# One kernel's attention stage, two chunks at a time: scores, state sums and value products of both chunks grouped by kind

## The chip, the cores and the metric

The kernel runs on one core of one Trainium2 chip. The metric is the device time of one execution in microseconds (us). Five engines of the core work side by side, each through its own instructions in order: TensorE (PE in the profile; PEld is its weight load), VectorE (DVE), ScalarE (ACT), GpSimd (POOL) and SyncE (SP), whose queue issues most of the DMAs here.

## What is computed

A gated linear attention feeds a gated feed-forward layer. Cut to what matters:

```
a = (a_re + i*a_im) * min(|a|, 0.999) / (|a| + 1e-6)
for t in range(768):                       # each of 4 batches, 8 heads, head size 48
    S = a[t][:, None] * S + outer(k[t], v[t])          # S complex, 48 x 48
    y[t] = q[t] @ real(S)
x = y rearranged to 3072 tokens x 384
h = x @ w_in                               # 384 -> 2048
out = (h * cos(h)) @ w_out                 # 2048 -> 384
```

## The kernel before

**Chunks and groups.** The 768 steps of a batch are cut into 6 chunks of 128 steps, 24 chunks in all. Two neighbouring chunks make a group, so there are 12 groups, 0 to 11. Groups 0 and 1 run by an order written out by hand. Groups 2 to 11 run in one loop, whose pass `n` holds group n's attention, group n's first product (tokens by `w_in`), the second product (by `w_out`) of group n-1, and the preparation of group n+1 (logs of the gates, their running sums over the chunk, angles, turned keys and queries).

**One chunk's attention.** `f_scores` (twice, four heads each) multiplies keys by queries into a PSUM tile `sc`; VectorE multiplies it by the causal mask into `atm`. `f_state` calls `state_sums`, 24 small products (three for each head) that fill the PSUM tile `sp`, and `state_next`, in which VectorE adds `sp` to the state of the chunk and multiplies by the decay `end` (two VectorE instructions; only one where nothing is carried into the chunk). The result is the state that the next chunk uses. `f_out` makes the chunk's values in the PSUM tile `yp`: for each pair of heads two matmuls on `atm` and, if the chunk has a state, two on the state; ScalarE then copies `yp` to `yT`. Nothing is carried into a batch's first chunk (this is the first chunk of groups 3, 6 and 9); a batch's last chunk makes no state sums (the second chunk of groups 2, 5, 8 and 11). `f_x` sends `yT` to a DRAM tile, `f_xt` brings it back as `xT`, the input of the first product.

**The logs' sums.** `log_steps` runs a chain over ScalarE and VectorE for group n+1: squares, logarithm, exponentials, a VectorE maximum-and-add into `pair`, a minimum into `lg`, a logarithm of `rs`, a subtraction into `lg`, its rounding `hi` on ScalarE and the rest `lo` on VectorE. `p_powers` (called through `prods`) sums `hi` and `lo` over the chunk by four matmuls into the PSUM tiles `lgs`; ScalarE takes exponentials of these.

**The second product** is done by seven block products (`seventh`, 8 matmuls each, in two halves of 4), in the order 0, 1, 3, 2, 5, 4, 6. `products(n-1, 0, 1)` is product 0 (PSUM tile `sum`), `products(n-1, 1, 2)` product 1 (`op`), `products(n-1, 2, 3)` product 3 (`sum`, with the left side `s2`). Product 5 follows in the same PSUM tile after ScalarE has copied product 3 out to `ot`.

**What sets the order.** `weave` takes lists of steps, each with a stretch (lo, hi) of the pass, spreads a list's steps evenly in its stretch, sorts all by place, and calls them. Every matmul goes through `matmul`, which puts it behind the one before it (line 692 of the profile): TensorE runs in exactly the woven order. In the loop the lists of VectorE and ScalarE are not fixed by hand (`Ordered.by_hand` is emptied at line 1814, except ScalarE's special functions, which are chained): the compiler's list scheduler orders them, and it was the same scheduler that filled the order seen in the trace. SP's queue is in the scheduler's order too, with a few DMAs put behind others (`behind`).

Before, `chunks(n)` has ten steps in the stretch 0 to 0.36: for each chunk two score halves, an empty step, and one step with `f_state` and `f_out`; then `f_x`, the load of `im` for group n+2 and `f_xt`; then the fetch of `end` and `v`. The logs' sums are not a list of their own: the second chunk's `f_out` calls them as `between`, ahead of its first pair of heads, or ahead of its third where the chunk is the last of a batch. Product 1's halves stand at 0.0975 and 0.1925 of the pass, one between the first chunk's scores and its sums, the other between the second chunk's score halves:

```
product 0 | sc sc | product 1 half | sp yp | sc | product 1 half | sc | sp (logs' sums) yp | product 3 ...
```

The PSUM pool `pa` has five banks; `sc`, `sp`, `yp`, `lgs`, the phases' sums and some tiles of the first product share it.

## Time and profile before

| | |
|---|---|
| median of 3 runs | 629.77 us (629.24 to 630.23) |
| the profiled execution | 629.86 us, span 628.1 us |
| granted TensorE clock | 0.998 |
| busy: PE, PEld, DVE, ACT | 608.1, 555.3, 531.8, 461.3 us |
| matmul records | 5057 |

The profile comes from one execution. Its page gives busy times by engine, the span in 40 slices, the chain that ended last, and groups of instructions; the trace behind it also answers who waited for whom, and lists instructions in order of time. A line of such a list reads: start, length, engine, line of the code, operation, output <- inputs, partitions and shape, count; in brackets the engine's idle time before it and what ended that. Neighbouring instructions of one form are merged into one line, so its length covers them all and the engine's pipelined ends overlap with the next line. Starts of neighbouring lines are therefore compared, not lengths. A matmul in full float32 is listed as two records: a score half of four heads is x8, a chunk's state sums x48, half of a block product x8.

### The profile page before, as it was taken

The page shows a single profiled execution, that of the slowest core. Times are in us where ns is not written, and L with a number is a line of the kernel's source. Part 1 is how long each engine was busy: PE and PEld are TensorE (multiplying, and loading weights), DVE is VectorE, ACT ScalarE, POOL GpSimd, SP SyncE. Part 2 cuts the span into 40 slices and gives each one's busy share as a digit, 9 for nine tenths or more (in the row PEclk, how much of TensorE's full clock was granted, in tenths as well). Part 3 has the DMA queues.
Part 4 walks back from the last instruction along what each step waited for, and adds up shares of the span by engine and source line. Part 5 has one row for each costly group of instructions (what it writes and reads, how often), then busy time and mean ns, then how long its engine had stood idle before and what let it go on. Part 6 is the DMA issues. An engine that isn't in the chain of part 4 may idle for free.

```text
span 628.1 us, 12990 instructions
## 1 busy us (share of the span) xinstructions
PE 608.1 (97%) x5057; PEld 555.3 (88%) x5057; DVE 531.8 (85%) x779; ACT 461.3 (73%) x832; POOL 28.5 (5%) x45
## 2 busy tenths in 40 slices
PE   8899999999999998998999999999999999999995
PEld 5788867776889998998999999998999999999995
DVE  6999989967898799899889989889889989982471
ACT  7888687286698597698598698598599598572440
POOL 4010110000000000000000000000000000000000
PEclk9999999999999999999999999999999999999999
DMA  9969574714937567486396496496496494371001
GB/s 235 257 185 226 166 214 79 201 46 107 226 69 187 152 148 202 125 180 176 102 223 179 111 220 175 105 218 166 121 222 174 110 228 125 104 176 52 27 0 32
DMA packets 237569, 95.04 MB, mean 151 GB/s; under 512 B 209501, under 2 KB 229726, under 8 KB 237498
## 3 DMA queue, kind: packets, MB, share of 16 engines
q1 hardware_dynamic: 229960, 68.51, 46.5%
q0 software_dynamic: 5824, 25.50, 13.1%
q8 instruction: 42, 0.69, 0.5%
q10 hardware_dynamic: 1714, 0.11, 0.2%
q14 instruction: 29, 0.24, 0.1%
HBM read 69.28 MB, written 24.81 MB: 150 GB/s over the span
## 4 chain that ended last, share of the span: by engine, by line
PE 55%; ACT 19%; DVE 13%; issue 5%; DMA 4%; SPq 2%; ACTq 0%; DVEq 0%
PE hp L692 20%; PE op L692 13%; PE sum L692 12%; PE hb L692 3%; ACT xT L681 2%; PE yp L692 2%; DVE tr L681 2%; PE phs L692 2%; ACT tan L712 2%; ACT rs L712 2%; ACT gate L712 2%; DMA kT<-moved 2%; ACT L708 2%; ACT lg L712 2%; DVE gate L681 2%
## 5 line engine op out<-in xcount | busy, mean ns | idle before, releaser
L712 ACT ACTIVATE gate<-hp,half_pi_b 128x512 f32<-128x512 f32 x96 | 68.7, 715 | 50.2 <-PE hp L692 30.3
L692 PE MATMUL hp<-xT,w_in 128*128 128x256 f32 (+1 forms) x492 | 104.9, 369 | 0.0
L692 PE MATMUL op<-w_out,gate 128*128 128x192 f32 (+1 forms) x464 | 102.3, 370 | 0.0
L692 PEld LDWEIGHTS hp<-xT,w_in 128*128 128x128 f32 x492 | 89.7, 190 | 12.6 <-issue 0.2
L692 PEld LDWEIGHTS op<-w_out,gate 128*128 128x128 f32 x464 | 78.7, 190 | 15.2 <-issue 0.4
L692 PE MATMUL hp<-xh,wh 128*128 128x256 f32 x342 | 60.8, 286 | 0.0
L681 ACT ACTIVATE xT<-hp 128x512 bf16<-128x512 f32 x96 | 60.0, 625 | 0.0
L692 PE MATMUL hp<-xl,wl 128*128 128x256 f32 x342 | 59.0, 281 | 0.0
L692 PE MATMUL sum<-w_out,gate 128*128 128x192 f32 x304 | 52.5, 326 | 0.0
L681 DVE SCALAR_TENSOR_TENSOR gate<-hp,gate 128x512 f32<-128x512 f32 x57 | 39.2, 688 | 13.0 <-ACT xT L681 12.7
L692 PE MATMUL sc<-qT,kT 96*128 96x128 f32 x384 | 49.6, 278 | 0.3 <-ACT qT L681 0.3
L692 PEld LDWEIGHTS hp<-xh,wh 128*128 128x128 f32 x342 | 49.5, 189 | 0.5
L692 PEld LDWEIGHTS sc<-qT,kT 96*128 96x128 f32 x384 | 46.7, 192 | 3.2 <-issue 1.9
L692 PEld LDWEIGHTS sum<-w_out,gate 128*128 128x128 f32 x304 | 49.5, 190 | 0.1
L692 PE MATMUL hb<-xx,wx 128*128 128x256 f32 x342 | 48.6, 282 | 0.0
L692 PEld LDWEIGHTS hp<-xl,wl 128*128 128x128 f32 x342 | 48.4, 188 | 0.0
L681 DVE TENSOR_TENSOR hp<-hp,gate 128x512 f32<-128x512 f32 x57 | 39.3, 693 | 6.8 <-PE hp L692 2.6
L692 PEld LDWEIGHTS hb<-xx,wx 128*128 128x128 f32 x342 | 44.0, 188 | 0.0
L681 ACT ACTIVATE gate<-hb 128x512 f32<-128x512 f32 x57 | 35.8, 628 | 10.8 <-PE hb L692 9.8
L692 PE MATMUL yp<-atm,v 128*48 128x128 f32 x352 | 33.8, 278 | 3.4 <-DVE atm L681 3.4
L681 DVE TENSOR_TENSOR gate<-hp,gate 128x512 f32<-128x512 f32 x39 | 26.2, 678 | 12.8 <-ACT xT L681 12.6
L681 DVE TENSOR_TENSOR atm<-sc,causal 128x512 f32<-128x512 f32 x48 | 32.3, 683 | 4.8 <-PE sc L692 4.8
(161 smaller groups left out, 1222.2 us busy)
## 6 DMA issues: line engine op xcount, KB each, us to landing
moved<-tr SPq DMA_DIRECT2D x20, 768.0 KB
raw<-in_moe_w_in_dram POOLq DMA_DIRECT2D x16, 768.0 KB, 5.7
raw<-in_moe_w_out_dram POOLq DMA_DIRECT2D x16, 768.0 KB, 5.3
kT<-moved SPq DMA_DIRECT2D x80, 96.0 KB
qT<-moved SPq DMA_DIRECT2D x20, 384.0 KB
k<-in_k_dram SPq DMA_DIRECT2D x24, 192.0 KB
q<-in_q_dram SPq DMA_DIRECT2D x24, 192.0 KB
v<-in_v_dram SPq DMA_DIRECT2D x24, 192.0 KB
```

The costliest lines, as they stand in the source:

```text
L681: ins = getattr(self.engine, op)(**kw)
L692: chain(nc.tensor.matmul(out, **kw), "tensor")
L708: chain(nc.scalar.preload_act_table_set(table))
L712: chain(nc.scalar.activation(func=func, **kw))
```

## The change

The step list `chunks` is split into lists of its own. In the pass, the four score halves of both chunks come first (places 0 to 0.05), then the state steps of both chunks (0.05 to 0.06), then the value products of both chunks and the `f_x`, `im`, `f_xt` step (0.06 to 0.09). The logs' sums become one step at 0.13 and are no longer called from within `f_out`. Product 1's halves move to 0.1125 and 0.1375, so that they stand before and after the logs' sums. The fetch of `end` and `v` keeps its place (0.342). On TensorE the order is then:

```
product 0 | sc sc sc sc | sp sp | yp yp | product 1 half | logs' sums | product 1 half | product 3 ...
```

The matmuls themselves, and every other instruction, stay as they are in number and form.

```diff
-    def f_out(n, between=lambda: None):
+    def f_out(n):
...
         for p in range(HH):
-            if p == (0 if n % NCH < NCH - 1 else 2):
-                between()
             for side in range(2):
...
-    def chunks(g):
-        for n in range(g * G, g * G + G):
-            for hh in range(2):
-                yield lambda n=n, hh=hh: f_scores(n, hh)
-            yield lambda: None
-            yield lambda n=n: (f_state(n), f_out(n, lambda: n % G and [t() for t in prods(g + 1)]))
+    def own(g):
+        return range(g * G, g * G + G)
+
+    def scores(g):
+        return [lambda n=n, hh=hh: f_scores(n, hh) for n in own(g) for hh in range(2)]
+
+    def states(g):
+        return [lambda n=n: f_state(n) for n in own(g)]
+
+    def outs(g):
+        for n in own(g):
+            yield lambda n=n: f_out(n)
         yield lambda: (f_x(g), g + 2 < NG and load(g + 2, ("im",), put=after_x), f_xt(g))
+
+    def fetches(g):
         if PEG < g + 1 < NG:
             yield lambda: (ends(g + 1), load(g + 1, ("v",), put=lambda **kw: behind(
                 nc.sync.dma_start(**kw), late["ends"])))
...
-        weave((mixes(n - 1, 1, 2), 0.0, 0.08), (logs(n + 1), 0.0, 0.02), (chunks(n), 0.0, 0.36),
+        weave((mixes(n - 1, 1, 2), 0.0, 0.08), (logs(n + 1), 0.0, 0.02), (scores(n), 0.0, 0.05), (states(n), 0.05, 0.06), (outs(n), 0.06, 0.09),
+              ([lambda: [t() for t in prods(n + 1)]], 0.13, 0.13), (fetches(n), 0.342, 0.342),
               (upper[2:] if plain else [], 0.0, 0.2), (products(n - 1, 0, 1), -0.02, -0.01),
-              (products(n - 1, 1, 2), 0.05, 0.24), (products(n - 1, 2, 3) if n < NG - 1 else [], 0.28, 0.36),
+              (products(n - 1, 1, 2), 0.1, 0.15), (products(n - 1, 2, 3) if n < NG - 1 else [], 0.28, 0.36),
```

## The prediction, on record before the changed kernel ran

> **What bounds the kernel now.** I read the page's shares first, then the waits of TensorE, then TensorE's and VectorE's instructions in order of time for one pass of the loop, then the same stretch in the other passes.

> ```profile
> span 628.1 us, 12990 instructions
> PE 608.1 (97%) x5057; PEld 555.3 (88%) x5057; DVE 531.8 (85%) x779; ACT 461.3 (73%) x832; POOL 28.5 (5%) x45
> PEclk9999999999999999999999999999999999999999
> ```

> ```profile
> PE yp L692 <- DVE atm L681: 3.4, 4, 1.1
> PE sum L692 <- ACT ot L681: 1.8, 4, 0.6
> PE lgs L692 <- DVE lo L681: 1.6, 3, 0.8
> ...
> PE lgs L692 <- ACT hi L733: 0.5, 1, 0.5
> ```

> TensorE is busy all the way (97%) at full clock (9 in every slice), so the program is TensorE's list plus its waits, and no wait of the first product (`hp`) for `xT` is among them. The rows give us in total, times, and the longest. What this change can remove is in the four rows: 3.4 us before value products, 1.6 + 0.5 us before the logs' sums, and 1.8 us before product 5 (`sum`), which waits until ScalarE has copied product 3 out. The second thing to know is how close VectorE runs behind. This is group 10's attention stage on TensorE:

> ```profile
> 513.57 1.95 PE L692 MATMUL sc<-qT,kT 96*128 96x128 f32 x16
> 515.35 1.47 PE L692 MATMUL op<-w_out,gate 128*128 128x192 f32 x8
> 516.75 0.88 PE L692 MATMUL sp<-v,ks 128*32 128x48 f32 x48
> 517.56 0.43 PE L692 MATMUL yp<-atm,v 128*48 128x128 f32 x4
> 517.82 0.39 PE L692 MATMUL yp<-qT,state 96*48 96x128 f32 x4
> ...
> 519.46 1.16 PE L692 MATMUL sc<-qT,kT 96*128 96x128 f32 x8
> 520.45 1.47 PE L692 MATMUL op<-w_out,gate 128*128 128x192 f32 x8
> 521.76 1.06 PE L692 MATMUL sc<-qT,kT 96*128 96x128 f32 x8
> 522.74 0.88 PE L692 MATMUL sp<-v,ks 128*32 128x48 f32 x48
> 523.55 0.44 PE L692 MATMUL lgs<-hi,exact 128*128 128x384 f32 x1
> ...
> 524.45 0.43 PE L692 MATMUL yp<-atm,v 128*48 128x128 f32 x4
> ...
> 526.35 2.87 PE L692 MATMUL sum<-t_s,gate 128*128 128x192 f32 x16
> ...
> 532.12 2.87 PE L692 MATMUL sum<-t_s,s 128*128 128x192 f32 x16 [0.30 <-ACT ot L681]
> ```

> and on VectorE over the same time:

> ```profile
> 515.23 0.68 DVE L681 SCALAR_TENSOR_TENSOR gate<-hp,gate 128x512 f32<-128x512 f32 x1
> 515.83 0.68 DVE L681 TENSOR_TENSOR atm<-sc,causal 128x512 f32<-128x512 f32 x1
> 516.42 0.68 DVE L681 TENSOR_TENSOR s<-gate 128x512 f32<-128x512 f32 x1
> 517.02 0.68 DVE L681 TENSOR_TENSOR atm<-sc,causal 128x512 f32<-128x512 f32 x1
> 517.63 0.68 DVE L681 TENSOR_TENSOR gate<-gate 128x512 f32<-128x512 f32 x1
> 518.23 0.95 DVE L681 SCALAR_TENSOR_TENSOR pair<-re,pair 128x768 f32<-128x768 f32 x1
> 519.09 0.55 DVE L681 TENSOR_SCALAR lg<-lg 128x768 f32<-128x768 f32 x1
> 519.56 0.54 DVE L681 SCALAR_TENSOR_TENSOR state<-sp,state 96x384 f32<-96x384 f32 x1
> 520.03 0.94 DVE L681 TENSOR_TENSOR lg<-lg,rs 128x768 f32<-128x768 f32 x1
> 520.90 0.54 DVE L681 TENSOR_TENSOR state<-state,end 96x384 f32<-96x384 f32 x1
> 521.36 0.68 DVE L681 TENSOR_TENSOR gate<-s,gate 128x512 f32<-128x512 f32 x1
> 522.15 0.96 DVE L681 SCALAR_TENSOR_TENSOR lo<-lg,hi 128x768 fp32r<-128x768 f32 x1
> ```

> No row has an idle time: VectorE is full from the last gate of the first product (515.23) on. It carries the masks (`atm`), the state, and the log chain (`pair`, `lg`, `lg`, `lo`) in one line. The first state is finished at 520.90 + 0.54 = 521.44, and its user, the second chunk's value products, comes at 524.45: three microseconds of cover, made by two score halves, half of product 1, the second state sums and the logs' sums. Group 10 has no wait in this stage; group 8, a batch's end without second state sums, has one, and group 9, whose first chunk opens a batch and carries nothing in, almost none:

> ```profile
> 419.43 1.95 PE L692 MATMUL sc<-qT,kT 96*128 96x128 f32 x16
> ...
> 429.64 0.43 PE L692 MATMUL yp<-atm,v 128*48 128x128 f32 x4 [0.96 <-DVE atm L681]
> ...
> 432.57 2.87 PE L692 MATMUL sum<-t_s,gate 128*128 128x192 f32 x16
> ```

> ```profile
> 466.89 1.95 PE L692 MATMUL sc<-qT,kT 96*128 96x128 f32 x16
> ...
> 470.88 1.08 PE L692 MATMUL yp<-atm,v 128*48 128x128 f32 x16
> 471.89 1.16 PE L692 MATMUL sc<-qT,kT 96*128 96x128 f32 x8
> ```

> **What goes.** The eight waits before `yp` and `lgs` (4 + 3 + 1) idle 3.4 + 1.6 + 0.5 = 5.5 us, and each costs a little more than its idle, since the pipeline refills: group 8's stage takes 432.57 - 419.43 = 13.14 us; group 10's 526.35 - 513.57 = 12.78 less one set of state sums (517.56 - 516.75 = 0.81) is 11.97; the difference is 1.17 for an idle of 0.96. So 5.5 + 8 x 0.2 = 7.1 us go, if nothing takes their place: the masks of the second chunk can now be made while state sums and the first value products run.

> The four waits before product 5 go too. ScalarE copies the second chunk's `yp` between the logs' sums and that point now; afterwards it has done so before. Their idle is 1.8 us; with the same refill 1.8 + 4 x 0.2 = 2.6; I take 2.5.

> Fewer changes of matmul form. After the change group 10 would take 32 score records at 1.78 for 16 (515.35 - 513.57), 3.56; a change to `sp` 0.09 (522.74 - 521.76 = 0.98 against 0.89 for half of 1.78); two state sums 1.62; two value products 1.80 and 1.90 (519.46 - 517.56 = 1.90, of which 0.1 is the change); half of product 1, 1.31 + 0.10 for its change (515.35 to 516.75 is 1.40); logs' sums 0.90 (524.45 - 523.55); the other half 1.31. Sum 12.59 against 12.78: 0.2 a group, in nine groups 1.8 us. [...]

> **What comes: a wait for the first state.** Scores of both chunks now come first, so VectorE gets four masks where it had two, ahead of the state; and the state's user comes earlier. Which of two ready instructions VectorE takes is the scheduler's choice. The rows show it taking, of what is ready, what stands earliest in the pass: the log chain (place 0.01) ahead of the state (0.126), and at 517.63 a subtraction of the mixes (place 0.15), when neither was ready. In the new pass the logs still stand at 0.01, scores to 0.044, `s` at 0.04, states at 0.0525. With the steps of the rows (a mask 0.60, `pair` 0.86, `lg` 0.47, the subtraction 0.87, the first state operation 0.47), VectorE's list becomes: mask 515.83, mask 516.43, mask or `s` 517.03 and 517.63, `pair` 518.23, `lg` 519.09, last mask 519.56, subtraction 520.16, state 521.03 and 521.50, finished 522.04. TensorE wants that state after 3.56 + 0.09 + 1.62 + 1.80 and the second chunk's first four records (517.82 - 517.56 = 0.26): 7.33 us after 513.57, at 520.90. It waits 1.1, with the semaphore 1.2 us. Behind the waiting `yp` everything on TensorE queues: the rest of the chunk, product 1, the logs' sums; ScalarE's copy to `yT` waits with it. By type of group: where the second state sums are missing (5, 8) TensorE comes 0.8 earlier and waits 2.0; where the first chunk opens a batch (3, 6, 9) its value products take 1.01 instead of 1.90 (471.89 - 470.88), TensorE comes 0.9 earlier, but the state is one operation, finished 0.46 earlier: 1.6. In 4, 7 and 10 it is 1.2. Sum 2 x 2.0 + 3 x 1.6 + 3 x 1.2 = 12.4. Group 2, with longer second products between, is not shown in such a form; between 0 and 2.0 I take 1.0, near group 10's. Group 11 prepares no logs and pays nothing. 13.4 us in all.

> **What moves at no cost.** `f_x`, five `im` loads and `xT` now stand ahead of the `re` loads on SP. The data arrive no later than before, and TensorE does not wait for `xT` today. If that cover were gone, `hp` would wait at the start of the first product. The logs' sums come after 3.56 + 0.09 + 1.62 + 3.70 + 1.41 = 10.38 us and the new wait 1.2, at 11.6; before at 9.98 (523.55). `lo` needs only 522.15 + 0.96 - 513.57 = 9.54, or a state's two operations later, so no wait is left there.

> **The sum.** 629.86 - 7.1 - 2.5 - 1.8 + 13.4 = 631.9 us. The profiled execution (span 628.1, 1.8 outside it) lies 0.1 above the median, 629.77, which changes nothing. [...]

> **The rivals.**

> *The state goes first.* If the scheduler sees the state sums ready before the log chain, the state is finished about 515.83 + 4 x 0.60 + 0.47 + 0.54 = 519.2, before TensorE asks. Then nothing takes the place of the old waits: 629.86 - 11.4 = 618.5, and about 2 back in groups 3 and 4, whose `lo` comes late (there the old waits were for `lo` and `hi`): 620.5. For it: the state operation at 519.56 went ahead of the subtraction. Against it: `pair` and `lg` are ready by 518.23 and stand earlier in the pass.

> *Only the subtraction gives way.* If at 520.16 it isn't ready yet, as it wasn't at 519.56, the state is done 0.87 earlier in eight groups: 631.9 - 7.0 = 624.9.

> *The masks come one step later.* If the scheduler believes the later scores unready at 517.63, it fills in the subtraction of the mixes as it does today, and state and masks are each 0.60 later. In eight groups that is 4.8: 636.7. It decides as soon as the third mask starts after 518.2 in group 10's time. This is the mechanism on the slow side, beside my own; waits of over 3 us it doesn't give.

> *Nothing to measure.* New waits equal to old ones in each type of group, 629.9.

> **How the numbers follow.** A measurement of this kernel tells 0.2%, 1.26 us, from no change: faster is under 628.5, slower over 631.0. My forecast has 0.43, with two to three us either way for group 2 and the early groups 3 to 5, whose VectorE rows come later than group 10's: 0.02 faster, 0.13 same, 0.28 slower. State first 0.22 and subtraction giving way 0.14, all faster; masks later 0.14, slower; nothing 0.07, same. Faster 0.38, same 0.20, slower 0.42. The forecast's own range is 629 to 634.5; the one for 8 in 10 reaches to the cases on both sides, 620 to 637.

> **What would show it.** Right: TensorE's waits list `yp` behind VectorE's `state`, eight or nine times with 1 to 2 us; `yp` behind `atm`, `lgs` behind `lo` and `sum` behind `ot` are gone or small; on VectorE the subtraction into `lg` stands ahead of the first state operation, and the last mask after `pair`. Wrong: `state` in front of `pair` or `lg`, or no wait of `yp` above 0.5 us; then the time is near 620. If `hp` or `phs` waits, a later chain has taken over that I held to be covered.

## The result, and the profile after

The changed kernel takes 637.46 us (median of 4 runs, 637.12 to 639.15); the kernel before, on the same chip, 630.00 (629.24 to 630.99). The ratio is 1.0123, with a 95% interval from 1.0100 to 1.0146: slower, by 7.5 us. The forecast was 631.9 with a range from 620 to 637, so the direction with the highest chance was right and the size lies just outside the range. The profiled execution took 637.12 us, of which 635.3 are its span.

The page of the changed kernel, its first lines:

```profile
span 635.3 us, 12981 instructions
...
PE 606.6 (95%) x5057; PEld 560.5 (88%) x5057; DVE 532.4 (84%) x779; ACT 460.2 (72%) x832; POOL 29.1 (5%) x45
...
PEclk9999999999999999998999999999999998999998
```

The work is the same (5057 matmuls) and TensorE's share fell from 97 to 95%. New are the slices with an 8 in the clock's row; the first two lie in groups 5 and 10, the third is the end of the program, behind the last matmul. TensorE's waits, in total, times, longest:

```profile
PE yp L692 <- DVE state L681: 16.1, 9, 3.0
...
PE sum L692 <- ACT ot L681: 0.9, 2, 0.5
...
PE yp L692 <- DVE atm L681: 0.3, 1, 0.3
```

This is the prediction's mechanism: the value products wait nine times for the first chunk's state. The waits for `lo` and `hi` are gone; what is left for `atm` is one of group 1, in the part ordered by hand. But the new wait is 16.1 us instead of the 13.4 that the prediction gives. Group 10 on TensorE:

```profile
518.06 3.74 PE L692 MATMUL sc<-qT,kT 96*128 96x128 f32 x32
521.73 1.56 PE L692 MATMUL sp<-v,ks 128*32 128x48 f32 x96
...
527.70 0.43 PE L692 MATMUL yp<-qT,state 96*48 96x128 f32 x4 [2.30 <-DVE state L681]
...
529.55 2.93 PE L692 MATMUL op<-w_out,gate 128*128 128x192 f32 x8
...
533.11 1.46 PE L692 MATMUL op<-w_out,gate 128*128 128x192 f32 x8
534.40 2.76 PE L692 MATMUL sum<-t_s,gate 128*128 128x192 f32 x16
```

TensorE asks for the state at 527.70 - 2.30 = 525.40, 7.34 us after the first score; the prediction had worked out 7.33. The state is what is late. The two rows of `op` are the two halves of one product with the same shape: 2.93 us in front, 1.46 behind. The first ran at half clock, as the windows below show. VectorE over the same time shows why the state is late:

```profile
519.56 1.28 DVE L681 TENSOR_TENSOR atm<-sc,causal 128x512 f32<-128x512 f32 x2
...
521.76 0.96 DVE L681 SCALAR_TENSOR_TENSOR pair<-re,pair 128x768 f32<-128x768 f32 x1 [0.32 <-ACT pair L712]
522.64 0.68 DVE L681 TENSOR_TENSOR atm<-sc,causal 128x512 f32<-128x512 f32 x1
523.24 0.55 DVE L681 TENSOR_SCALAR lg<-lg 128x768 f32<-128x768 f32 x1
523.70 0.68 DVE L681 TENSOR_TENSOR atm<-sc,causal 128x512 f32<-128x512 f32 x1
524.30 0.95 DVE L681 TENSOR_TENSOR lg<-lg,rs 128x768 f32<-128x768 f32 x1
525.17 0.54 DVE L681 SCALAR_TENSOR_TENSOR state<-sp,state 96x384 f32<-96x384 f32 x1
525.64 0.68 DVE L681 TENSOR_TENSOR gate<-gate 128x512 f32<-128x512 f32 x1
526.24 0.94 DVE L681 SCALAR_TENSOR_TENSOR lo<-lg,hi 128x768 fp32r<-128x768 f32 x1
527.11 0.54 DVE L681 TENSOR_TENSOR state<-state,end 96x384 f32<-96x384 f32 x1
```

The state stands behind `pair`, the last mask and the subtraction into `lg`, as forecast; its first operation starts 7.11 us after the first score, where the prediction's list has 7.46. Its two operations were forecast next to each other. Between them stand a subtraction of the mixes (525.64, 0.60 to the next start) and `lo` (526.24, 0.87), so the state is finished at 527.11 + 0.54 = 527.65, 9.59 us after the first score; the prediction has 8.47.

The half clock can be read from windows over the wait and over the work behind it. The columns are the stretch, its length, busy time of PE, PEld, DVE, ACT and POOL, the granted TensorE clock, and the DMAs; first group 5, then 8, then 10, each with the wait in the first row:

```profile
281.00:284.30 3.30, 0.35 (x8) 0.09 (x2) 3.30 (x7) 3.24 (x5) 0.00 (x0) 0.86 0.58 210
284.30:290.00 5.70, 5.69 (x37) 5.29 (x37) 4.19 (x6) 3.88 (x8) 0.76 (x1) 0.50 0.14 32
427.50:431.90 4.40, 1.53 (x28) 1.27 (x24) 4.40 (x8) 4.34 (x7) 0.00 (x0) 1.00 0.58 182
431.90:437.00 5.10, 5.08 (x48) 4.90 (x49) 3.95 (x5) 3.12 (x8) 0.72 (x1) 1.00 0.36 59
525.00:527.70 2.70, 0.41 (x8) 0.15 (x4) 2.70 (x6) 2.66 (x6) 0.00 (x0) 1.00 0.54 222
527.70:532.50 4.80, 4.80 (x37) 4.45 (x38) 3.22 (x5) 1.48 (x3) 0.72 (x1) 0.65 0.29 51
```

Behind the wait of group 5 (2.96 us) the clock is 0.50, behind that of group 10 (2.30) 0.65, behind that of group 8 (2.89) it stays at 1.00. From the end of the wait to product 3 group 5 takes 292.21 - 284.31 = 7.90 us where group 8 takes 437.00 - 431.92 = 5.08 for the same matmuls; group 10 takes 534.40 - 527.70 = 6.70 where group 7 takes 388.15 - 383.07 = 5.08. That is 2.8 + 1.6 = 4.4 us, more than half of the whole loss.

### The profile page after: what moved, and what is told of

It is laid out like the page before. It is cut to its first block, busy times and chain, and to the rows that moved or that the text cites. A ratio compares the mean times of both kernels' runs of the same rounds, so it can differ in the third digit from the quotient of the medians.

```text
span 635.3 us, 12981 instructions
## 1 busy us (share of the span) xinstructions
PE 606.6 (95%) x5057; PEld 560.5 (88%) x5057; DVE 532.4 (84%) x779; ACT 460.2 (72%) x832; POOL 29.1 (5%) x45
## 4 chain that ended last, share of the span: by engine, by line
PE 60%; DVE 18%; ACT 14%; issue 4%; DMA 3%; SPq 1%; DVEq 0%; ACTq 0%
PE op L692 19%; PE hp L692 18%; PE sum L692 13%; PE yp L692 3%; PE hb L692 3%; ACT gate L712 3%; ACT xT L681 3%; DVE lg L681 3%; DVE gate L681 2%; DVE tr L681 2%; DVE atm L681 2%; PE phs L692 2%; ACT L708 2%; DVE pair L681 2%; DMA kT<-moved 2%
## 5 line engine op out<-in xcount | busy, mean ns | idle before, releaser
L692 PE MATMUL op<-w_out,gate 128*128 128x192 f32 (+1 forms) x464 | 105.4, 379 | 0.0
L692 PE MATMUL hp<-xT,w_in 128*128 128x256 f32 (+1 forms) x492 | 104.9, 370 | 0.0
L692 PEld LDWEIGHTS hp<-xT,w_in 128*128 128x128 f32 x492 | 89.7, 190 | 12.5 <-issue 0.2
L692 PEld LDWEIGHTS op<-w_out,gate 128*128 128x128 f32 x464 | 81.6, 195 | 17.1 <-issue 2.0
L692 PE MATMUL hp<-xh,wh 128*128 128x256 f32 x342 | 60.8, 286 | 0.0
L692 PE MATMUL hp<-xl,wl 128*128 128x256 f32 x342 | 59.0, 281 | 0.0
L681 ACT ACTIVATE xT<-hp 128x512 bf16<-128x512 f32 x96 | 59.0, 614 | 0.0
L692 PE MATMUL sum<-w_out,gate 128*128 128x192 f32 x304 | 52.5, 326 | 0.0
L692 PEld LDWEIGHTS hp<-xh,wh 128*128 128x128 f32 x342 | 49.5, 189 | 0.5
L692 PEld LDWEIGHTS sum<-w_out,gate 128*128 128x128 f32 x304 | 49.5, 190 | 0.1
L692 PE MATMUL hb<-xx,wx 128*128 128x256 f32 x342 | 48.6, 282 | 0.0
L692 PEld LDWEIGHTS hp<-xl,wl 128*128 128x128 f32 x342 | 48.4, 188 | 0.0
L681 DVE SCALAR_TENSOR_TENSOR gate<-hp,gate 128x512 f32<-128x512 f32 x57 | 39.1, 686 | 9.9 <-ACT xT L681 9.6
L681 ACT ACTIVATE gate<-hb 128x512 f32<-128x512 f32 x57 | 35.3, 619 | 16.3 <-PE hb L692 15.3
L681 DVE TENSOR_TENSOR hp<-hp,gate 128x512 f32<-128x512 f32 x57 | 39.5, 694 | 8.6 <-PE hp L692 4.2
L692 PE MATMUL yp<-qT,state 96*48 96x128 f32 x304 | 31.1, 283 | 16.1 <-DVE state L681 16.1
L692 PE MATMUL sc<-qT,kT 96*128 96x128 f32 x384 | 45.5, 276 | 0.3 <-ACT qT L681 0.3
L692 PEld LDWEIGHTS sc<-qT,kT 96*128 96x128 f32 x384 | 44.5, 192 | 1.0 <-ACT qT L681 0.5
L692 PEld LDWEIGHTS hb<-xx,wx 128*128 128x128 f32 x342 | 44.0, 189 | 0.0
L681 ACT ACTIVATE ot<-sum 128x192 f32<-128x192 f32 x39 | 12.6, 323 | 36.3 <-PE sum L692 35.4
L681 DVE TENSOR_TENSOR gate<-hp,gate 128x512 f32<-128x512 f32 x39 | 26.3, 677 | 13.1 <-ACT xT L681 12.9
```

The lines of the kernel that those rows point to most:

```text
L681: ins = getattr(self.engine, op)(**kw)
L692: chain(nc.tensor.matmul(out, **kw), "tensor")
```

## The experiments

The prediction's own reading (Theory A) is that VectorE reaches the first state too late, because the log chain stands ahead of it. Its rivals are named in the expectations. Each kernel was timed next to the kernel before, and the ratio is to those runs.

**Logs behind the states.** In the changed kernel the log chain moves from the front of the pass to a place behind the states; TensorE's order is the changed kernel's.

```diff
-(logs(n + 1), 0.0, 0.02)
+(logs(n + 1), 0.06, 0.062)
```

> The changed kernel, with the log chain traced behind the state steps (place 0.061 instead of 0.01), so that VectorE's list holds the first state ahead of the chain's subtraction; TensorE's order stays. Theory A (TensorE waits for the first state because VectorE makes it late, and the clock falls after the longest of these waits): the state is ready about 7.3 us into the stage where TensorE asks for it at 7.0, so the waits of yp for state fall from 16.1 us to under 4 us, no slice shows a lower clock, and the time is 616 to 622 us. Rival B (what counts is that nothing stands between the scores and the value products on TensorE, whichever operation of VectorE comes first): still above 630 us. Rival C (the clock alone, about 4 us of the 7.4): 632 to 634 us.

Measured: 625.24 us (624.85 to 625.65), ratio 0.9933 (0.9917 to 0.9950), clock 0.998. TensorE's waits:

```profile
PE yp L692 <- DVE state L681: 2.7, 4, 1.6
PE sum L692 <- ACT ot L681: 2.3, 4, 1.2
PE lgs L692 <- DVE lo L681: 1.8, 4, 0.8
```

With one number changed the wait for the state falls from 16.1 to 2.7 us and the kernel is faster than both. Rivals B and C fall with that. It isn't as fast as expected, since 2.3 us before product 5 and 1.8 before the logs' sums came back. The loss is the place of the log chain on VectorE, not the grouping on TensorE.

**Product 1 as cover.** Both halves of product 1 stand between the two chunks' value products, so TensorE asks for the state 2.6 us later.

```diff
-(products(n - 1, 1, 2), 0.1, 0.15)
+(products(n - 1, 1, 2), 0.066, 0.074)
```

> The changed kernel, with both halves of product 1 moved between the first and the second chunk's value products (places 0.068 and 0.072 instead of 0.1125 and 0.1375); VectorE's order nearly stays. Theory A: 2.6 us of work stand ahead of the matmul that waits for the state, so waits of 0.7 to 3.0 us become 0 to 0.5, clock full, logs' sums without a wait: 614 to 620 us. Rival B' (VectorE is the bound of the stage, so cover at one place is waited for at another, at the logs' sums or product 3): above 628 us. Rival C: 632 to 634 us.

Measured: 628.57 us (627.30 to 632.04), ratio 0.9988 (0.9978 to 0.9997).

```profile
PE sum L692 <- ACT ot L681: 6.5, 7, 1.6
...
PE yp L692 <- DVE state L681: 0.2, 1, 0.2
```

The wait for the state goes completely, and a wait of 6.5 us before product 5 takes its place: Theory A is right on the wait and wrong on the time. The time is that of Rival B' (above 628), and so is the mechanism, though the place is product 5 and the wait is for ScalarE. The cover seems to have been needed twice: where it stood, it gave ScalarE time between the logs' sums and product 5.

**The waits filled.** In groups 4, 5, 7, 8 and 10, where the wait was longest, TensorE gets twelve small matmuls on constant tiles, ahead of the second chunk's value products. They add work that the result doesn't need.

```diff
+ps = pa.tile([C, 512], F32, tag="a", name="fill")
+for _ in range(12):
+    matmul(ps[:, 0:C], lhsT=exact, rhs=alls, start=True, stop=True)
```

> The changed kernel plus 12 idle matmuls (128x128, not part of the computation, their result is not used) between the two chunks' value products in groups 4, 5, 7, 8 and 10, where the wait for the state is 2.3 to 3.0 us. They take about 1 us of the wait and add no work elsewhere. If the lower clock of groups 5 and 10 comes from the length of TensorE's idle time: idle falls by 1 us in these groups, the clock stays full, and the time falls by the 4 us that the two groups lost, to 632 to 634 us. If the lower clock has another cause: 637 us, two stages still at half clock.

Measured: 634.75 us (632.40 to 638.08), ratio 1.0087 (1.0054 to 1.0119). The idle time before `yp` is 8.1 us, half of 16.1, with no wait over 1.4. The clock over the five runs goes with the time: 0.999 in the run of 632.40, 0.993 in those of 637.08 and 638.08. The profiled run has half-clock stretches behind waits of 1.36 and 1.30 us in groups 5 and 8 (clock 0.70 in 284.40 to 290.00 and 0.67 in 430.80 to 436.00). The time lies between the two that were expected: the run at full clock has the 632 of the first, the profiled one the two half-clock stretches of the second. So with this much filling the clock stayed full in one run and not in the profiled one.

**Scores alone.** In the kernel before, the four score halves stand at the front of the pass, and nothing else is regrouped.

```diff
+def scores(g):
+    return [lambda n=n, hh=hh: f_scores(n, hh) for n in range(g * G, g * G + G) for hh in range(2)]
...
             for hh in range(2):
-                yield lambda n=n, hh=hh: f_scores(n, hh)
+                yield lambda: None
...
-(chunks(n), 0.0, 0.36),
+(scores(n), 0.0, 0.05), (chunks(n), 0.0, 0.36),
```

> The kernel before, with only the four score halves brought to the front of the pass (places 0 to 0.05); sums, value products, logs' sums and product 1 keep their old places. Theory A: the masks are made early and half of product 1, state sums and logs' sums still stand ahead of the second chunk's value products; no wait for the state above 0.5 us, the old waits of yp for masks are gone (3.4 us): 622 to 628 us. Rival B'' (bringing four masks to the front pushes the log chain back, and that is what costs): waits of the logs' sums for lo, 632 us or more.

Measured: 630.58 us (628.94 to 635.06), ratio 1.0013 (1.0001 to 1.0024). The waits before `yp` for `atm` fall from 3.4 us to 0.3, but 2.7 for `state` take their place; those for `lo` stay (1.6 before, 1.7 now), and half of product 1 no longer splits the scores. That is no gain, and neither expectation holds: Theory A had 622 to 628 and no wait for the state, Rival B'' 632 or more. In the profiled run, the slowest of the eleven, half clock follows the longer wait for the state, 2.27 us in group 5: from 294.66 on four records of the value products take 0.64 to 0.67 us, where they take 0.39 at full clock.

**Logs behind and half of product 1 as cover.** One half of product 1 between the value products, one ahead of the logs' sums.

```diff
-(logs(n + 1), 0.0, 0.02)
+(logs(n + 1), 0.06, 0.062)
...
-(products(n - 1, 1, 2), 0.1, 0.15)
+(products(n - 1, 1, 2), 0.05, 0.13)
```

> The variant with the logs behind the states, and product 1's halves at 0.07 and 0.11: one half between the two chunks' value products, the other ahead of the logs' sums. Theory A (TensorE idles for the first state because its user comes before VectorE's list reaches it; 1.3 us of other work in between removes what the logs' move left): yp behind state falls from 2.7 us to under 0.3, the logs' sums come later and don't wait for lo, 622 to 624.5 us. Rival D (the cover is paid back before product 5, since the exponentials of the logs' sums and what follows them on ScalarE now come later and the copy ot behind them): sum behind ot rises from 2.3 to 4 us or more and the time stays at 625 to 627.

Measured: 626.75 us (626.13 to 627.03), ratio 0.9934 (0.9917 to 0.9950): Rival D.

```profile
PE sum L692 <- ACT ot L681: 5.3, 5, 1.8
...
PE lgs L692 <- DVE lo L681: 0.6, 1, 0.6
```

The wait for the state is down to 0.2 us. What the state and `lo` give back, product 5 takes. Why ScalarE copies `ot` so late is seen in its list in the variant with the logs behind, group 4; product 3 has run on TensorE from 238.54, product 5 starts at 245.09 after a wait of 1.20:

```profile
240.25 1.28 ACT L708 ACT_TABLE_LOAD   x1
241.86 0.84 ACT L712 ACTIVATE tan<-tan 128x768 f32<-128x768 f32 x1 [0.32 <-DVE tan L681]
243.98 0.84 ACT L733 ACTIVATE hi<-tan 128x768 fp32r<-128x768 f32 x1 [1.28 <-DVE tan L681]
244.73 0.31 ACT L681 ACTIVATE ot<-sum 128x192 f32<-128x192 f32 x1
```

ScalarE isn't busy: it waits 1.28 us for VectorE in the rounding `hi` of `tan`, and the copy, 0.31 us, stands behind that.

**The carries behind.** To take the rounding out of the way, the carries move behind product 3. The fetch at 0.342 now sends out the decays' last rows ahead of their correction, which the carries hold; the program's own test of its data then takes its second, general path. This variant changes the computation, and its time, 2051.06 us, says nothing on the question. The first 625 us of its trace, the first path, can be read.

```diff
-(carries(n + 1), 0.336, 0.34)
+(carries(n + 1), 0.38, 0.384)
```

> The variant with the logs behind the states, and the carries (the sum across chunks and the rounding of tan) at 0.38 instead of 0.336, behind product 3. In the trace of that variant ScalarE's copy ot of product 3 stands behind the rounding hi<-tan, which waits for VectorE. Theory E (the wait before product 5 is this queue on ScalarE, not the copy of yp): sum behind ot falls from 2.3 us to under 0.5, and unless phs waits longer for the later hi, the time is 622 to 624. Rival F: phs and the turned keys come later by as much as product 5 gains; waits of phs rise by over 2 us and the time is 625 to 628.

In those 625 us no wait before product 5 is left, and new ones appear elsewhere:

```profile
PE hp L692 <- ACT xh L681: 10.4, 5, 2.1
PE sc L692 <- DMA qT<-moved: 5.6, 3, 2.2
...
PE yp L692 <- DVE state L681: 2.9, 4, 1.8
```

Both theories hold a part: with the step gone from in front of the copy, product 5 doesn't wait, and moving the whole step behind makes others late. The first product waits for `xh`, a part of its input that ScalarE makes, and the scores wait for the queries (16.0 us in the first two rows).

**The logs behind in the kernel before.** The log chain behind the first chunk's state, and no regrouping.

```diff
-(logs(n + 1), 0.0, 0.02)
+(logs(n + 1), 0.13, 0.132)
```

> The kernel before, with the logs alone at 0.13 instead of 0.0, that is behind the first chunk's state, and nothing regrouped. Theory A (what the regrouping gains is fewer changes of form and fewer waits for masks; the logs' place alone gives nothing): the log chain comes later and the logs' sums, which still stand ahead of the second chunk's value products, wait for lo; 630 to 636. Rival G (the logs in front of state and masks are the whole loss, and the grouping is worth nothing): 624 to 627, like the regrouped kernel with the logs behind.

Measured: 637.57 us (633.77 to 639.26), ratio 1.0124 (1.0104 to 1.0144). The waits before the logs' sums, 2.1 us in the kernel before, are 8.1 in two rows:

```profile
PE lgs L692 <- DVE lo L681: 4.2, 8, 0.8
PE lgs L692 <- ACT hi L733: 3.9, 4, 1.6
```

The time lies just above the 630 to 636 of Theory A; the profiled run is the fastest of the five, 633.77. Rival G falls: the late log chain pays only with the regrouping, which moves the logs' sums behind both chunks.

**A longer state.** Two multiplications by 1 behind the state's second operation.

```diff
             vector.tensor_tensor(out=new, in0=new, in1=end, op=ALU.mult)
+            if n // G > 2:
+                for _ in range(2):
+                    vector.tensor_scalar(out=new, in0=new, scalar1=1.0, scalar2=None, op0=ALU.mult)
```

> The changed kernel with two more VectorE operations (a multiplication by 1 of 96 x 384, 0.47 us each, the values unchanged) behind the state's second one, in the chunks of groups 3 to 11 that add to a state already there. In 4, 5, 7, 8 and 10 the first state is then finished later by 0.94 us and by whatever the scheduler puts between, in 3, 6 and 9 not. Theory H (the clock falls to half when TensorE has stood idle for long enough, so longer waits make more half-clock stretches): yp behind state rises to 20 us or more, stretches at half clock behind most of the waits of 4, 5, 7, 8 and 10, and the time is 645 or more, that is more than the 4 to 8 us of longer waiting above 637.5. Rival I (the two half-clock stretches have nothing to do with the length of the wait): the same two or so stretches, 641 to 645 us, the waits alone.

Measured: 656.57 us (654.87 to 659.87), ratio 1.0427 (1.0395 to 1.0459), clocks from 0.974 to 0.979.

```profile
PE yp L692 <- DVE state L681: 28.1, 10, 5.9
```

The windows of group 5 (wait of 5.89 us) and 6 (1.09), each from before the wait to its end, and from there to product 3:

```profile
286.00:290.80 4.80, 0.00 (x0) 0.00 (x0) 4.59 (x10) 4.60 (x8) 0.00 (x0) 0.67 0.14 55
290.80:296.00 5.20, 5.17 (x39) 4.79 (x40) 4.17 (x6) 1.16 (x2) 0.75 (x1) 0.65 0.31 60
334.00:339.30 5.30, 4.26 (x130) 3.82 (x129) 5.30 (x10) 5.20 (x8) 0.74 (x1) 1.00 0.53 121
339.30:344.40 5.10, 5.05 (x48) 4.86 (x49) 5.10 (x9) 5.00 (x11) 0.76 (x1) 1.00 0.38 104
```

All five waits over 4 us (4.48, 5.89, 4.32, 4.92, 4.32) are followed by half clock: the windows behind those of groups 4, 5, 7 and 8 have 0.70, 0.65, 0.72 and 0.50, and behind that of group 10 four records of the value products take 0.65 us instead of 0.39. None of the waits near 1.1 is; the windows over those of groups 6 and 9 have 1.00. From the wait's end to product 3 the five groups take 6.58, 6.76, 6.56, 7.62 and 6.70 us instead of 5.08: 8.8 us, where the changed kernel lost 4.4. Longer waiting (28.1 - 16.1 = 12.0) and lost clock (4.4 more) make 16.4 of the 17.8 by which its span, 653.1, is longer. Theory H holds for this kernel: the longer waits came with more half clock, five stretches for two.

**The copy's place, with cover.** The variant with both edits, and product 3's second half just ahead of the rounding in the pass, so that ScalarE's hand-made order has the copy in front of it.

```diff
-(products(n - 1, 2, 3) if n < NG - 1 else [], 0.28, 0.36)
+(products(n - 1, 2, 3) if n < NG - 1 else [], 0.28, 0.357)
```

> The variant with the logs behind and a half of product 1 on each side of the second value products, and product 3's second half at 0.338 instead of 0.34, so that ScalarE's copy ot is listed between the arctangent and the rounding of tan instead of behind both; nothing leaves its engine. Theory E (the wait before product 5 is ScalarE waiting in that rounding for VectorE): sum behind ot falls from 5.3 us to under 1, and the time to 620 to 622.5. Rival F (what is put behind ot makes phs late by as much): phs behind hi or tan rises by over 2 us, 625 to 627.

Measured: 621.04 us (620.43 to 622.53), ratio 0.9845 (0.9814 to 0.9876), the fastest version found.

TensorE is busy for 98% of a span of 619.8 us.

```profile
PE sum L692 <- ACT ot L681: 0.3, 1, 0.3
```

One wait each is left for `lo` (0.4 us) and for the state (0.2). Theory E holds, and `phs` waits no longer than before.

**The copy's place, without cover.** The same edit on the variant with the logs behind.

> The variant with the logs behind, and the same earlier place for product 3's second half. Theory E: sum behind ot falls from 2.3 us to under 0.5, 622 to 624; the waits for the state (2.7) and for lo (1.8) stay, so it is slower than the variant with both. Rival F: 625 to 627, with phs later.

Measured: 622.22 us (621.39 to 623.59), ratio 0.9862 (0.9831 to 0.9893): no wait before product 5 is listed any more, those for the state (2.3) and `lo` (1.8) stay. The half product as cover removes most of these 4.1 us and saves little over 1 us of time (the two intervals overlap). It splits the value products: group 10's stage, without a wait in either, takes 516.35 - 503.80 = 12.55 us with it and 521.99 - 509.78 = 12.21 in the variant with the logs behind. And from product 3 to product 5 the groups 3 to 5 take 16.6 us with it and 15.6 without.

**The state's two operations together.** In the changed kernel the subtraction of the mixes is tied behind the state's second operation; the scheduler then moves `lo` behind it too.

```diff
-            vector.tensor_tensor(out=new, in0=new, in1=end, op=ALU.mult)
+            late["state"] = vector.tensor_tensor(out=new, in0=new, in1=end, op=ALU.mult)
...
         late["mixed"] = vector.tensor_tensor(out=mix[name], in0=mix[a], in1=mix[b], op=ALU.subtract)
+        if name == "s3" and g + 1 in (4, 5, 7, 8, 10):
+            behind(late["mixed"], late["state"])
```

> The changed kernel, with the subtraction of the mixes tied behind the state's second operation in 4, 5, 7, 8 and 10; the list scheduler then puts the state's two operations next to each other and lo behind them. In the trace of the changed kernel the mixes' subtraction (0.60) and lo (0.87) stand between the two in 7, 8 and 10, and neither does in 4 and 5. Theory A (these 1.47 us are what the prediction's list lacked): the waits of 7, 8 and 10 fall from 2.30, 2.89 and 2.30 to 0.8, 1.4 and 0.8, those of 4 and 5 stay at 2.4 and 3.0, yp behind state is 11 to 12.5 us in all, the half-clock stretch of 10 goes, and the time is 630.5 to 633.5. Rival J (the second operation starts when it does because of something else, and what is moved away is replaced): waits over 14.5 us, 636 to 638.

Measured: 635.93 us (634.50 to 636.59), ratio 1.0074 (1.0049 to 1.0098). VectorE in group 10, and the waits:

```profile
522.54 0.94 DVE L681 TENSOR_TENSOR lg<-lg,rs 128x768 f32<-128x768 f32 x1
523.41 0.54 DVE L681 SCALAR_TENSOR_TENSOR state<-sp,state 96x384 f32<-96x384 f32 x1
523.99 0.55 DVE L681 TENSOR_TENSOR state<-state,end 96x384 f32<-96x384 f32 x1
524.63 0.96 DVE L681 SCALAR_TENSOR_TENSOR lo<-lg,hi 128x768 fp32r<-128x768 f32 x1
```

```profile
PE yp L692 <- DVE state L681: 11.3, 9, 3.0
PE sum L692 <- ACT ot L681: 2.8, 4, 0.8
```

This is the order that the prediction had written down, and the waits are what that order gives: 0.59 in group 7, 1.37 in 8 and 0.58 in 10, while 4 and 5 keep 2.43 and 2.97 and group 5 its half clock (four records of the value products in 0.64 us instead of 0.39). The expected sum of the waits came, the expected time, 630.5 to 633.5, didn't. In the traces 1.9 us more before product 5 took a part of the gain back, and a larger part is lost where none of this plays: from the start of the last matmul to the end of the span this run takes 9.5 us, the changed kernel 7.0 and the kernel before 7.0. Up to that matmul it is 3.7 us ahead of the changed kernel, at the end of the span 1.2. Why the end takes longer wasn't traced; in the fastest version above it takes 9.3.

**The copy's place in the kernel before.** The same edit of product 3's stretch, nothing regrouped.

> The kernel before, its attention stage as it was, with product 3's second half at 0.338 instead of 0.34 alone, so that ScalarE's copy ot is listed ahead of the rounding of tan. It tells how much of the gain of the variant with both edits belongs to the copy's place and how much to the regrouping. Theory A (the copy's place takes the four waits before product 5 and no more, and the regrouping with the logs behind is worth the rest): sum behind ot falls from 1.8 us to under 0.5, ratio 0.995 to 0.998, 627.5 to 630. Rival K (the copy's place is most of the gain and the regrouping adds little): ratio 0.99 or less, 624.5 or less.

Measured: 628.41 us (627.06 to 631.37), ratio 0.9937 (0.9911 to 0.9963). No wait before product 5 is listed, those for `atm` (3.4), `lo` (1.6) and `hi` (0.5) are as before. The ratio lies between the two expectations, 0.995 or more for Theory A and 0.99 or less for Rival K. So of the 1.55% that the fastest version gains, some 0.6% belongs to the copy's place, which has nothing to do with the change, and the rest to the grouping with its log chain and cover: 0.9% by this run, 0.7% by the variant with the logs behind, which has no other place for the copy. The interval of the fastest version doesn't meet that of this run.

## Why the prediction was wrong in size

Its terms, against what the two traces give for the passes of the loop (a stage is the time from the first score to product 3):

| term | predicted | measured |
|---|---|---|
| old waits before `yp` and `lgs` | -7.1 | -6.2 |
| waits before product 5 | -2.5 | -2.3 |
| fewer changes of form | -1.8 | -4.3 |
| new wait for the state | +13.4 | +16.8 |
| clock | not in the sum | +4.4 |
| sum | +2.0 | +8.4 |

The spans differ by 7.2; 0.45 of the remaining 1.2 lies ahead of the loop, the rest wasn't traced further. Two steps failed: the list of VectorE that gave the new wait, and the clock, put at nothing. By size it is the clock: without its 4.4 us the time would be 633. That the four terms ahead of it come so near to the forecast together, +4.0 for +2.0, is in part luck, since the new wait was taken 3.4 us too low and the changes of form 2.5 us too low.

*What goes* was right. The stages of groups 3 to 10 before, less those of their kind without a wait (12.78, 11.97 and 12.23), give 5.0 us, pass 2 another 1.2. One of the eight waits, 0.3 us, belongs to group 1, which the change doesn't touch; what the waits cost beyond their idle time, the prediction's refill, was 1.0 us for the other seven, not 1.6 for eight. In single rows before, group 6's `lo` product starts 0.74 us behind the `hi` product with an idle time of 0.30, and group 10's 0.28 without one: 0.16 more than the idle time. From product 3 to product 5 nine groups took 50.30 us before and take 48.04 now.

*The changes of form* were worth more than the rows had seemed to say. Group 10 without a wait takes 12.78 us before and 12.21 in the variant with the logs behind: 0.57. Group 9 gives the same (12.23 and 11.66). Where the second state sums are missing it is 0.44: those sums cost 0.81 us apart and 0.68 behind the first ones (12.55 less 11.87, groups 10 and 8 of the fastest version), so groups 5 and 8 without a wait would take 11.97 before and 11.53 after. In eight groups that is 4.3 us. The saving read from single neighbouring rows, 0.2 a group, was too small. Group 11 loses two such changes and gains only 0.03, so no fixed price for a change comes out of these runs. The fastest version, whose half product splits the value products again, takes 12.55.

*The new wait* is the first step that failed, and it failed by VectorE's list, in the prediction's words "subtraction 520.16, state 521.03 and 521.50". TensorE's arrival was right to 0.01 us, and from the state's end to the waiting `yp` it is 0.05 (527.65 to 527.70 in group 10), where the prediction adds up to 0.1 for the semaphore. The state's first operation came behind what the prediction had put ahead of it; its second one doesn't follow at once, as the prediction had it. In groups 7, 8 and 10 the mixes' subtraction and `lo`, 1.47 us, stand between; the run that ties the subtraction behind brings their waits down by 1.71, 1.52 and 1.72 us, so this cause is shown. In groups 4 and 5 it is the log chain's subtraction (0.87 us) that stands between, which the list has ahead of both. There VectorE reaches `pair` late: in group 5 6.35 us after the first score (281.03 - 274.68), where the list has 4.66 (518.23 - 513.57), since the last gate of the first product and two operations of the mixes stand among the masks; in group 4 it also idles 0.50 us for `pair` of ScalarE. This is read from the lists, and no run tests it. The prediction named this for groups 3 to 5 as a spread of two to three us and left it out of the sum. Groups 3, 6 and 9 wait less than forecast, 0.66, 1.25 and 1.10 for 1.6, and group 2 waits 0.19 for 1.0. Stages less their kind without a wait (12.21, 11.53 and 11.66) give 21.0 us for the groups 3 to 10; without the clock's 4.4 it is 16.6, and group 2 adds 0.2. That is 0.7 more than the 16.1 us of idle time; for the new waits the prediction counted no refill.

```profile
279.97:283.38 3.41, 1.38 (x26) 1.12 (x22) 3.41 (x6) 3.35 (x5) 0.00 (x0) 1.00 0.75 227
426.74:430.15 3.41, 2.29 (x49) 1.97 (x39) 3.41 (x6) 3.35 (x5) 0.62 (x1) 1.00 0.59 167
430.15:433.57 3.42, 1.65 (x28) 1.49 (x28) 3.39 (x6) 2.24 (x5) 0.00 (x0) 1.00 0.17 68
525.73:529.14 3.41, 1.44 (x26) 1.44 (x28) 3.41 (x6) 2.27 (x5) 0.00 (x0) 1.00 0.24 99
```

TensorE idles 3.41 - 1.38 = 2.03 us in group 5's cell and 1.97 in group 10's, and the next cell runs at half clock. Group 8's longer wait is divided between two cells, 1.12 and 1.77, and the clock stays. In the loops of the traces, but for the filled kernel, the one with the carries behind and the copy's place in the kernel before, half clock follows nine cells, each with 1.97 us of idle time or more: two in the changed kernel, five with the longer state (waits of 4.32 to 5.89 us), one each in scores alone (2.27) and with the state's two operations together (2.97). In the changed kernel and the kernel before it follows no cell with 1.77 or less. Of the eight waits of 2.27 to 2.97 us in the changed kernel and these last two variants, four were followed by half clock and four weren't; in the changed kernel this went by how they fell on the grid (no cell of groups 4 and 7 has over 1.60). In the filled kernel two cells with 1.36 and 1.30 us of idle time were followed by half clock; they hold the twelve small matmuls, and why the clock fell there stays open.

*The rivals.* The state didn't go first: in group 10 it was `pair`, `lg` and the subtraction that did. "Only the subtraction gives way" happened by half in groups 4 and 5, whose first state operation went ahead of the subtraction and the second behind it; this gained nothing. With the logs' place changed, "The state goes first" happened in part, at 625.2 instead of 620.5, since waits of `ot` and `lo` came with it. "The masks come one step later", with 636.7, is near the measured time but isn't what happened: in group 10 the masks start 0.8 us earlier than in the prediction's list.

## What to carry to other kernels

Where a wait is forecast from another engine's list, ask of each dependent pair of instructions whether the scheduler will fill the space between them, and with what; and then whether TensorE's idle time is long enough to cost clock on top (here, 1.97 us or more within one cell of 3.41). A regrouping on one engine moves the deadlines on all others: here its own gain (4.3 us of form changes, 8.5 of old waits) was real, and it took one number in the log chain's place, and one in the copy's, to keep it. A wait of TensorE behind a short copy on ScalarE (here of 0.31 us) may be a wait for what stands in front of the copy; read that engine's list before adding cover.

## What was not expected of the hardware

TensorE's clock was granted at half for 3.41 and 6.83 us after idle times of 2.30 and 2.96 us, at the price of 1.6 and 2.8 us, while idle times of 2.44, 2.89 and another of 2.30 us cost nothing: what counted was the idle time within one cell of a grid of 3.41 us, 1.97 us or more. In group 10 the half clock begins at 529.14, 1.44 us behind the wait's end. Two things don't fit this measure. In the kernel with the filled waits half clock came behind 1.36 and 1.30 us of idle time, and its time differs from run to run (632.40 to 638.08 us). And ahead of the loop, from about 36 to 47 us after the start, the profiled runs of two variants (product 1 as cover, scores alone) have 10.2 us of half clock (the windows from 30 to 38 us have 0.87 and 0.92, those from 38 to 46 have 0.50) behind cells with only some 0.7 and 0.8 us of idle time. What sets it off there stays open.
